# Attention backward with cached K and V: gradient stores moved to the SyncE queue, and three quarters of K transposed by DMA

## The chip, the cores and the metric

The kernel runs on one core of a Trainium2 chip. The metric is the device time of one execution in microseconds; for the kernel before, it is the median of three runs. A profile is one further execution, recorded by the hardware profiler. Engines are called PE (TensorE matmul), PEld (TensorE weight load), DVE (VectorE), ACT (ScalarE), POOL (GpSimd) and SP (SyncE, which here only issues DMAs). "SPq" in a profile line is SP's instruction queue.

## The reference

Two independent attention blocks, A and B, share one output gradient, and each is computed forward and backward. Everything is bfloat16: 8 batches of 96 queries, model width 640, 32 heads of width 128, 512 cached keys and values per head and batch.

```python
def ref(x, k_cache, v_cache, wq, wo):            # for A and for B
    q = (x @ wq).reshape(B, Sq, H, Dh).transpose(0, 2, 1, 3)
    scores = einsum("bhqd,bhkd->bhqk", q, k_cache) * Dh ** -0.5
    p = softmax(scores)
    o = einsum("bhqk,bhkd->bhqd", p, v_cache)
    return o.transpose(0, 2, 1, 3).reshape(B, Sq, H * Dh) @ wo
out = concatenate([ref(A...), ref(B...)], -1)
# returned: out, and for each block the gradients of x, k_cache, v_cache, wq, wo
```

The gradients of k_cache and v_cache are as large as the caches: 8 x 32 x 512 x 128 values each, 33.6 MB, twice for two blocks. Loading K and V and storing dK and dV is most of the traffic.

## The kernel before

Work is cut into 2 blocks x 32 heads x 8 batches = 512 items, one item being one head of one batch. The items run through a software pipeline of *ticks*: in each tick, PE, DVE, ACT and POOL each do one stage of several neighbouring items. An emitter collects closures under a tick and a slot, sorts them, and calls them in that order, so the order of the program is written out by hand; the compiler behind it may still reorder instructions, except those wrapped in `pinned(...)`, which keep the order of the program on their engine. `OFF` gives the tick of each stage relative to the item's own tick: K load -5, V load -3, K^T -3, V^T 0, the score matmul S (stage s2) 3, dV (s4) 4, dP (s6) 6, dK (s7) 7, dQ (s8) 8.

Loads, transposes and stores go by pairs of batches (`NB = 2`), 256 KB each. The steps that the change and the prediction touch:

- `c_ld` (L266) loads K_sb (7 buffers) or V_sb (5 buffers) of a pair from SP. A K buffer comes free when stage s8 of the pair seven earlier has read it.
- `c_xt` (L275) transposes a loaded pair by a crossbar DMA from SP, into VT (4 buffers) for every pair and into KT (2 buffers) for those pairs whose K^T is not made on PE.
- `c_s1` (L285, L287) makes K^T of one item on PE instead: four 128 x 128 transposes into PSUM (kT_ps) and a copy by DVE into KT_pe. `k_on_pe` chooses: pairs 0 and 2 of a head's four, all of head 0 of a block, and all of head 1 of the first block.
- `c_s2a` (L298) multiplies Q with K^T into S_ps; softmax follows on DVE (L300), ACT (L310), DVE (L320) and POOL (L329, P_sb).
- `c_s4` (L389) and `c_s7` (L432) make dV and dK of an item in PSUM, and ACT copies each (L392, L435) into dV_sb or dK_sb, which hold a pair and have 3 buffers each.
- `c_st` (L398) stores such a pair. It is issued by POOL, whose DMAs go through the software queue, and it is pinned there together with POOL's P_sb (L329) and prod (L407). A dV store is emitted two ticks after the dV stage of the pair's first item, a dK store likewise.
- `c_s6` (L417) reads V^T for dP.

Around these stand work per head (projections, transposes of weights, dwo and dwq: L210, L216, L243, L258, L455, L470, L490), whose weight loads and gradient stores POOL issues, and group work (L512): after every five or six heads, the output and dx products of the group are spread over 9 ticks each.

Of the kernel before, what the change touches and what calls it, by code (L numbers as in the profile page):

```python
# [44 lines left out]
OFF = dict(ldk=-5, ldv=-3, kt=-3, vt=0, s2=3, s3=3, s4=4, s5=5, s6=6, s7=7, s8=8)  # L45
# [5 lines left out]
SLOTS = dict(LOAD=0, S2A=5, S2B=5.5, S1=6, S8=10, S7=20, S5=30, S4=40, S6=50, S3A=52, S3B=53, S5B=54, HEAD=SL_HEAD, GRP=SL_GRP)  # L51


def build_block(tc, em, tick0, blk, x, kc, vc, wq, wo, g_all, out_all, dx, dk, dv, dwq, dwo, ident, ones, pools, HG=6, first=True, groups=None):
    nc = tc.nc
# [7 lines left out]
    KC = Sk // 128  # L63
    NB = 2
# [38 lines left out]
    SB = {}  # L103
    HS = pools["HS"]
    CS = pools["CS"]
# [5 lines left out]
    def pinned(ins):  # L111
        return tc.keep_in_program_order(ins)
# [68 lines left out]
    def pA(h):  # L181
        def f():
            start = first and h == 0
            if h % 2 == 0:
                wq_p = hd.tile([128, DC, 256], BF16, name="wq_p", bufs=2)
                with nc.allow_non_contiguous_dma(reason="wq slice of two heads"):
                    if start:
                        nc.sync.dma_start(wq_p[:], wq_v[:, :, h * 128:(h + 2) * 128])
                    else:
                        pinned(nc.gpsimd.dma_start(wq_p[:], wq_v[:, :, h * 128:(h + 2) * 128]))  # L190
            else:
                wq_p = HS[(blk, h - 1)]["wq_p"]
            HS[(blk, h)] = dict(wq_p=wq_p, wq_h=wq_p[:, :, (h % 2) * 128:(h % 2 + 1) * 128])
        return f

    def pA2(h):
        def f():
            wo_h = hst.tile([128, D], BF16, name="wo_h", bufs=HG + 3)
            ld = nc.gpsimd.dma_start(wo_h[:], wo[h * 128:(h + 1) * 128, :])
            if not (first and h == 0):  # L200
                pinned(ld)
            HS[(blk, h)]["wo_h"] = wo_h
        return f
# [23 lines left out]
    def pC(h, which, si):  # L227
        def f():
            st = HS[(blk, h)]
            (t0, w) = tsplits[si]  # L230
            if which == 0:
                dst = st["QT_h"]
                lhs = lambda c: st["wq_h"][:, c, :]
                rhsT = S["xT"]
                sc = scale
            else:
                dst = st["dOT_h"]
                lhs = lambda c: st["woT_h"][:, c * 128:(c + 1) * 128]
                rhsT = S["gT"]
                sc = None  # L240
            q_ps = bank([128, w], F32, "q_ps")
            for c in range(DC):
                nc.tensor.matmul(q_ps[:], lhs(c), rhsT[:, c, t0:t0 + w], start=(c == 0), stop=(c == DC - 1))  # L243
            evac(EV["pC%d%d" % (which, si)], dst[:, t0:t0 + w], q_ps[:], sc)
        return f
# [16 lines left out]
    def c_ld(h, b, n, bufs):  # L262
        def f():
            src = kc if n == "K" else vc
            X = kvp.tile([128, NB, KC, 128], BF16, name=n + "_sb", bufs=bufs)
            nc.sync.dma_start(X[:], src[b:b + NB, h].rearrange("b (p c) d -> p b c d", c=KC))  # L266
            for i in range(NB):
                st = CS.setdefault((blk, h, b + i), {})
                st[n + "_sb"], st[n + "_all"] = X[:, i], X
        return f  # L270

    def c_xt(h, b, name, bufs):
        def f():
            XT = kvp.tile([128, NB * KC, 128], BF16, name=name, bufs=bufs)
            nc.sync.dma_start_transpose(XT[:], CS[(blk, h, b)][name[0] + "_all"][:].rearrange("p a c d -> p (a c d)"))  # L275
            for i in range(NB):
                CS[(blk, h, b + i)][name] = XT[:, i * KC:(i + 1) * KC].rearrange("p c k -> p (c k)")
        return f
# [116 lines left out]
    def c_st(h, b, which):  # L395
        def f():
            dst = dv if which == "v" else dk
            pinned(nc.gpsimd.dma_start(dst[b - 1:b + 1, h].rearrange("b (p c) d -> p b (c d)", c=KC), SB.pop((blk, h, b // 2, which))[:]))  # L398
        return f

    def c_s5b(h, b):
# [144 lines left out]
    NTS = len(tsplits)  # L546

    def k_on_pe(h, b):
        return (b // NB) % 2 == 0 or h == 0 or (first and h == 1)

    SX = pools["SX"]
    for g in range(NG):
        h0 = GH0[g]
        for hh in range(groups[g]):
            h = h0 + hh
            c0t = tick0 + h * B
            if not (first and h == 0):
                em.add(c0t + HK["pA"], 54.6, pA(h))
                em.add(c0t + HK["pA2"], 54.6, pA2(h))
            em.add(c0t + HK["pB"], SL_HEAD, pB(h))  # L560
            fh = first and h == 0
            p0, p1, d1, d0, late = HK["pC0"], HK["pC1"], HK["pD1"], HK["pD0"], 0
            if fh:
                p1, d1, d0, late = [3, 3], 3, 4, 7
            elif h == 0:
                p0, p1, d1, d0, late = [-2, 2], [0, 3], 3, 4, 7
            for si in range(NTS):
                em.add(c0t + p0[min(si, 1)], SL_HEAD, pC(h, 0, si))
                em.add(c0t + p1[min(si, 1)], SL_HEAD + late, pC(h, 1, si))
            em.add(c0t + d1, SL_HEAD + (8 if late else 0), pD(h, 1))  # L570
            em.add(c0t + d0, SL_HEAD, pD(h, 0))
            for b in range(B):
                ct = c0t + b
                if b % NB == 0:
                    em.add(tick0 - 12 if first and h == 0 and b == 0 else ct + OFF["ldk"], SLOTS["LOAD"], c_ld(h, b, "K", 7))
                    em.add(ct + OFF["ldv"], SLOTS["LOAD"], c_ld(h, b, "V", 5))
                    if not k_on_pe(h, b):
                        em.add(ct + OFF["kt"], SLOTS["LOAD"] + 1, c_xt(h, b, "KT", 2))
                    em.add(ct + OFF["vt"], SLOTS["LOAD"] + 1, c_xt(h, b, "VT", 4))
                if k_on_pe(h, b):  # L580
                    em.add(ct + 2, SLOTS["S1"], c_s1(h, b))
                em.add(ct + OFF["s2"], SLOTS["S2A"], c_s2a(h, b))
                em.add(ct + OFF["s2"], SLOTS["S2B"], c_s2b(h, b))
                em.add(ct + OFF["s3"], SLOTS["S3A"], c_s3a(h, b))
                em.add(ct + OFF["s3"], SLOTS["S3B"], c_s3b(h, b))
                em.add(ct + OFF["s5"], SLOTS["S5B"], c_s5b(h, b))
                if b % 2 == 1:
                    em.add(ct + OFF["s4"] + 1, 54.3, c_st(h, b, "v"))
                    em.add(ct + OFF["s7"] + 1, 54.3, c_st(h, b, "k"))
                em.add(ct + OFF["s4"], SLOTS["S4"], c_s4(h, b))  # L590
                for i, o in enumerate(("s8", "s7", "s5", "s4")):
                    SX.setdefault(ct + OFF[o], [None] * 4)[i] = (blk, h, b)
                em.add(ct + OFF["s6"], SLOTS["S6"], c_s6(h, b))
                em.add(ct + OFF["s7"], SLOTS["S7"], c_s7(h, b))
            hk = HK if first or h < H - 1 else dict(HK, qA0=13, qB=[14, 15], qA1=16, qD=[(19, 0, 2), (19, 2, 4), (19, 4, 5)])
            em.add(c0t + hk["qA0"], SL_HEAD, qA(h, 0))
            for di in range(len(wsplits)):
                em.add(c0t + hk["qB"][di], SL_HEAD + 1, qB(h, di))
            em.add(c0t + hk["qA1"], SL_HEAD, qA(h, 1))
            for (k_, c_lo, c_hi) in hk["qD"]:  # L600
                if c_lo < DC and h % 2 == 1:
                    em.add(c0t + k_, SL_HEAD + 2, qD(h, c_lo, min(c_hi, DC)))
        cLg = tick0 + (h0 + groups[g] - 1) * B + B - 1
        gs0 = max(3, (GSPREAD0 * groups[g]) // HG)
        gs1 = max(3, (GSPREAD1 * groups[g]) // HG)
        if not first and g == NG - 2:
            gs0, gs1 = 9, 9
        if g == 0:
            em.add(cLg + OFF["s5"] - 2, SL_LOAD, setup_acc)
        subs = [(0, t, gi) for t in range(TT) for gi in range(len(gsplits))] + [(1, t, gi) for t in range(TT) for gi in range(len(gsplits))]  # L610
        n_out = TT * len(gsplits)
        for i, (which, t, gi) in enumerate(subs):
            if which == 0:
                tk = cLg + OFF["s5"] + 2 + (i * gs0) // n_out
            else:
                tk = cLg + OFF["s8"] + 2 + gs0 - 3 + ((i - n_out) * gs1) // n_out
            em.add(tk, SL_GRP, gU(g, which, t, gi))
# [124 lines left out]
```

## Time and profile before

| | before |
|---|---|
| time, three runs | 1693.32, 1705.34, 1706.98 us (median 1705.34) |
| span of the profiled execution | 1699.8 us (the page gives no other time of that execution) |
| mean granted TensorE clock | 0.998 |
| busy: PE, ACT, DVE, POOL | 1675.7, 1405.2, 1329.8, 1040.3 us |
| moved by DMA | 423.05 MB, 249 GB/s in the mean |
| of these on the hardware queue (SP) / the software queue (POOL) | 242.08 MB / 177.35 MB |
| dV and dK stores, from issue to landing | 5.2 and 5.3 us (median), 256 each |
| K and V loads, from issue to landing | 4.9 to 5.3 us (median), 128 of each kind |
| V^T and K^T by DMA, from issue to landing | 6.1 us (256) and 5.2 us (122) |

A row of the profile's groups reads: line, engine, operation, what it writes and reads, shapes, count, then busy us in all and mean ns of one, then idle time before it and who ended it. A busy PE counts the whole duration of pipelined matmuls, which overlap, so the cost of one is better read from start to start. The DMA share counts a packet from its start to its end, also while it waits for another queue's packets; it can exceed 1.

### The profile page before, as it was taken

To read this page: it belongs to the slowest core of one execution; us is meant where nothing else is said; L and a number is where in the kernel's file an instruction comes from. 1 tells how busy PE (TensorE), PEld (TensorE's weight loads), DVE (VectorE), ACT (ScalarE), POOL (GpSimd) and SP (SyncE) were. 2 spreads that over 40 slices of the span, in tenths; PEclk is the share of its full clock that TensorE was granted. 3 is DMA by queue.
4 is the path that set the end of the run, shared out by engine and by line. 5 is a ranking of instruction groups with operands and counts; after the bars stand their busy time and mean duration, and the time that the engine had idled before them with its cause. 6 is when DMAs were issued, how large, how long until landed. Compare 5 with 4: busy or idle time off the path is not lost.

```text
span 1699.8 us, 56567 instructions
## 1 busy us (share of the span) xinstructions
PE 1675.7 (99%) x22024; PEld 1343.8 (79%) x22024; DVE 1329.8 (78%) x3052; ACT 1405.2 (83%) x3518; POOL 1040.3 (61%) x1747
## 2 busy tenths in 40 slices
PE   8999999999999999999999999999999999999999
PEld 7877778778778778777778877887788778778876
DVE  6887678878788878787778876787788778878877
ACT  6998889869869869878768998897799679878975
POOL 3676567646647647656566764675576557656754
PEclk9999999999999999999999999999999999999999
DMA  9999999999999999999999999999899989999994
GB/s 256 252 259 250 258 225 260 262 242 243 262 221 252 268 238 259 225 251 237 281 256 269 273 270 248 238 289 248 218 261 276 237 221 261 281 217 240 263 247 141
DMA packets 600429, 423.05 MB, mean 249 GB/s; under 512 B 419360, under 2 KB 557984, under 8 KB 600160
## 3 DMA queue, kind: packets, MB, share of 16 engines
q1 hardware_dynamic: 546576, 242.08, 72.2%
q0 software_dynamic: 53584, 177.35, 32.7%
q8 instruction: 173, 2.83, 0.7%
q14 instruction: 96, 0.79, 0.2%
HBM read 161.09 MB, written 159.12 MB: 188 GB/s over the span
## 4 chain that ended last, share of the span: by engine, by line
PE 89%; DMA 4%; ACT 3%; issue 1%; DVE 1%; POOL 0%; SPq 0%; DVEq 0%; ACTq 0%; POOLq 0%
PE q_ps L243 12%; PE o_ps L512 12%; PE dwo_ps L470 6%; PE dV_ps L389 6%; PE dK_ps L432 6%; PE S_ps L298 6%; PE dP_ps L417 6%; PE dwq_ps L490 6%; PE x_ps L340 5%; PE x_ps L365 5%; PE dst_ps L346 5%; PE x_ps L359 5%; PE kT_ps L285 3%; PE n_ps L258 3%; PE nat_ps L455 2%; DMA VT<-V_sb 1%
## 5 line engine op out<-in xcount | busy, mean ns | idle before, releaser
L329 POOL TENSOR_SCALAR P_sb<-E_sb,rinv 96x512 bf16<-96x512 bf16 x512 | 352.6, 689 | 567.8 <-DVE rinv L320 559.2
L310 ACT ACTIVATE E_sb<-S_ps,negm 96x512 bf16<-96x512 f32 x512 | 351.0, 686 | 187.6 <-DVE negm L300 181.9
L421 DVE SCALAR_TENSOR_TENSOR dS_sb<-dP_ps,dl_ps,P_sb 96x512 bf16<-96x512 f32 x512 | 382.1, 746 | 60.9 <-PE dl_ps L419 54.6
L300 DVE TENSOR_REDUCE negm<-S_ps 96x1 f32<-96x512 f32 x512 | 347.6, 679 | 50.9 <-PE S_ps L298 46.6
L435 ACT ACTIVATE dK_sb<-dK_ps 128x512 bf16<-128x512 f32 x512 | 302.1, 590 | 63.4 <-PE dK_ps L432 56.5
L392 ACT ACTIVATE dV_sb<-dV_ps 128x512 bf16<-128x512 f32 x512 | 311.6, 609 | 0.0
L378 ACT ACTIVATE PT_sb<-x_ps 128x384 bf16<-128x384 bf16 x512 | 253.1, 494 | 0.0
L512 PEld LDWEIGHTS <-OD 128*128 128x128 bf16 x1536 | 132.2, 98 | 100.4 <-issue 1.0
L398 POOL DMA_DIRECT2D out_dram<-dV_sb x256 | 194.9, 761 | 11.8 <-issue 8.6
L398 POOL DMA_DIRECT2D out_dram<-dK_sb x256 | 195.0, 762 | 9.1 <-issue 4.4
L389 PE MATMUL dV_ps<-dOnat_h,P_sb 96*128 96x128 bf16 x2048 | 198.2, 219 | 0.8 <-DVE dOnat_h L160 0.6
L417 PE MATMUL dP_ps<-VT,dOT_h 128*96 128x512 bf16 x512 | 195.4, 382 | 3.0 <-DMA VT<-V_sb 3.0
L432 PE MATMUL dK_ps<-Qnat_h,dS_sb 96*128 96x128 bf16 x2048 | 198.1, 219 | 0.1
L407 POOL TENSOR_TENSOR prod<-OD,dOT_h 128x96 bf16<-128x96 bf16 x512 | 184.2, 360 | 13.8 <-ACT OD L375 12.6
L348 DVE COPY dST_sb<-dst_ps 128x384 bf16<-128x384 bf16 x512 | 177.1, 346 | 10.5 <-PE dst_ps L346 10.3
L365 PE MATMUL x_ps<-ident,P_sb 96*128 96x96 bf16 x2048 | 172.0, 205 | 0.8 <-POOL P_sb L329 0.3
L359 PE MATMUL x_ps<-PT_sb,V_sb 128*128 128x96 bf16 x2048 | 172.3, 206 | 0.2 <-ACT PT_sb L378 0.2
L346 PE MATMUL dst_ps<-ident,dS_sb 96*128 96x96 bf16 x2048 | 172.3, 206 | 0.2 <-DVE dS_sb L421 0.2
L340 PE MATMUL x_ps<-dST_sb,K_sb 128*128 128x96 bf16 x2048 | 171.0, 206 | 1.3 <-ACT dK_sb L435 0.8
L375 ACT ACTIVATE OD<-x_ps 128x192 bf16<-128x192 f32 (+1 forms) x515 | 167.9, 326 | 3.9 <-PE x_ps L340 3.9
L320 DVE RECIPROCAL rinv<-rowsum 96x1 f32<-96x1 f32 x512 | 79.9, 156 | 106.0 <-ACT E_sb L310 100.4
L340 PEld LDWEIGHTS <-K_sb 128*128 128x128 bf16 x2048 | 131.1, 98 | 25.1 <-issue 1.6
(84 smaller groups left out, 3744.4 us busy)
## 6 DMA issues: line engine op xcount, KB each, us to landing
out_dram<-dV_sb POOLq DMA_DIRECT2D x256, 256.0 KB, 5.2
out_dram<-dK_sb POOLq DMA_DIRECT2D x256, 256.0 KB, 5.3
K_sb<-in_A_k_cache_dram SPq DMA_DIRECT2D x128, 256.0 KB, 5.3
V_sb<-in_A_v_cache_dram SPq DMA_DIRECT2D x128, 256.0 KB, 5.2
K_sb<-in_B_k_cache_dram SPq DMA_DIRECT2D x128, 256.0 KB, 5.0
V_sb<-in_B_v_cache_dram SPq DMA_DIRECT2D x128, 256.0 KB, 4.9
out_dram<-dwo_sb POOLq DMA_DIRECT2D x63, 160.0 KB, 4.8
out_dram<-dwq_sb POOLq DMA_DIRECT2D x31, 320.0 KB, 6.1
```

The costliest lines, as they stand in the source:

```text
L300: nc.vector.tensor_reduce(negm[:], S_ps[:], axis=AX.X, op=ALU.max, negate=True)
L310: nc.scalar.activation(E_sb[:], st["S_ps"][:], ACT.Exp, bias=st["negm"][:], scale=1.0, accum_out=rowsum[:])
L329: pinned(nc.gpsimd.tensor_scalar(P_sb[:], st["E_sb"][:], st["rinv"][:], 0.0, op0=ALU.mult, op1=ALU.add))
L340: nc.tensor.matmul(dQT_ps, st["K_sb"][:, c, :], st["dST_sb"][:, c * Sq:(c + 1) * Sq], start=(c == 0), stop=(c == KC - 1))
L389: nc.tensor.matmul(dV_ps[:, c * 128:(c + 1) * 128], P_sb[:, c * 128:(c + 1) * 128], hs["dOnat_h"][:, b * 128:(b + 1) * 128], start=True, s ...
L392: nc.scalar.activation(SB[(blk, h, b // 2, "v")][:, b % 2], dV_ps[:], ACT.Identity, scale=1.0)
L398: pinned(nc.gpsimd.dma_start(dst[b - 1:b + 1, h].rearrange("b (p c) d -> p b (c d)", c=KC), SB.pop((blk, h, b // 2, which))[:]))
L417: nc.tensor.matmul(dP_ps[:], hs["dOT_h"][:, tok], st["VT"], start=True, stop=True)
L421: nc.vector.scalar_tensor_tensor(dS_sb[:], dP_ps[:], dl_ps[:, 0:1], st["P_sb"][:], op0=ALU.subtract, op1=ALU.mult)
L432: nc.tensor.matmul(dK_ps[:, c * 128:(c + 1) * 128], dS_sb[:, c * 128:(c + 1) * 128], hs["Qnat_h"][:, b * 128:(b + 1) * 128], start=True, s ...
L435: nc.scalar.activation(SB[(blk, h, b // 2, "k")][:, b % 2], dK_ps[:], ACT.Identity, scale=1.0)
L512: nc.tensor.matmul(o_ps[:], src[:, t * 128:(t + 1) * 128], rhs, start=(hh == 0), stop=(hh == groups[g] - 1))
```

## The change

The dV and dK stores are issued by SP, on its hardware queue, instead of POOL. In the emitter they get a slot right behind the loads and transposes of their tick, and loads, transposes and stores are all pinned, so SP issues them in the written order: V load, K load, K^T, dK store, V^T, dV store for each pair. `k_on_pe` keeps only pair 0 of a head on PE (and the same whole heads as before), so three quarters of a head's K^T come by DMA, 183 transposes instead of 122, and KT gets three buffers.

```diff
@@ c_ld
-            nc.sync.dma_start(X[:], src[b:b + NB, h].rearrange("b (p c) d -> p b c d", c=KC))
+            pinned(nc.sync.dma_start(X[:], src[b:b + NB, h].rearrange("b (p c) d -> p b c d", c=KC)))
@@ c_xt
-            nc.sync.dma_start_transpose(XT[:], CS[(blk, h, b)][name[0] + "_all"][:].rearrange("p a c d -> p (a c d)"))
+            pinned(nc.sync.dma_start_transpose(XT[:], CS[(blk, h, b)][name[0] + "_all"][:].rearrange("p a c d -> p (a c d)")))
@@ c_st
-            pinned(nc.gpsimd.dma_start(dst[b - 1:b + 1, h].rearrange("b (p c) d -> p b (c d)", c=KC), SB.pop((blk, h, b // 2, which))[:]))
+            pinned(nc.sync.dma_start(dst[b - 1:b + 1, h].rearrange("b (p c) d -> p b (c d)", c=KC), SB.pop((blk, h, b // 2, which))[:]))
@@ k_on_pe
-        return (b // NB) % 2 == 0 or h == 0 or (first and h == 1)
+        return b // NB == 0 or h == 0 or (first and h == 1)
@@ the loop over items
                     if not k_on_pe(h, b):
-                        em.add(ct + OFF["kt"], SLOTS["LOAD"] + 1, c_xt(h, b, "KT", 2))
+                        em.add(ct + OFF["kt"], SLOTS["LOAD"] + 1, c_xt(h, b, "KT", 3))
                     em.add(ct + OFF["vt"], SLOTS["LOAD"] + 1, c_xt(h, b, "VT", 4))
...
                 if b % 2 == 1:
-                    em.add(ct + OFF["s4"] + 1, 54.3, c_st(h, b, "v"))
-                    em.add(ct + OFF["s7"] + 1, 54.3, c_st(h, b, "k"))
+                    em.add(ct + OFF["s4"] + 1, SLOTS["LOAD"] + 1.5, c_st(h, b, "v"))
+                    em.add(ct + OFF["s7"] + 1, SLOTS["LOAD"] + 1.5, c_st(h, b, "k"))
```

## The prediction

> **What bounds the kernel now.** I read the page's busy line, the row of slices and the chain first, then the waits of PE, ACT and the SP queue, then windows of single heads.
>
> ```profile
> PE 1675.7 (99%) x22024; PEld 1343.8 (79%) x22024; DVE 1329.8 (78%) x3052; ACT 1405.2 (83%) x3518; POOL 1040.3 (61%) x1747
> ...
> DMA  9999999999999999999999999999899989999994
> ...
> PE 89%; DMA 4%; ACT 3%; issue 1%; DVE 1%; POOL 0%; SPq 0%; DVEq 0%; ACTq 0%; POOLq 0%
> ```
>
> PE sets the time: it is busy for 99% of the span and holds 89% of the chain. POOL, from which the change takes work, is on no path. The DMA row of 9s is a warning for a change that adds DMA work, but a weak one: a packet counts as busy while it waits, and packets of two queues overlap.
>
> ```profile
> PE dP_ps L417 <- DMA VT<-V_sb: 3.0, 2, 2.4
> ...
> PE S_ps L298 <- DMA KT<-K_sb: 2.1, 1, 2.1
> ```
>
> PE's waits (total us, times, longest) name a late transpose for only 5.1 us in all. So DMA is hidden now; how much room is left must be read from stretches of the run.
>
> The 64 heads are not alike. Taking the first dP matmul of each head as its mark, a head without group work (L512) takes 21 or 24 us in turn, and the two heads that carry it take about 33 and 30. Windows of two neighbouring heads and, first, of the stretch in which only the SP queue moves data (columns: window, its length, then busy us and instructions of PE, PEld, DVE, ACT, POOL, then PE clock, DMA share, GB/s):
>
> ```profile
> 17.00:24.00 7.00, 6.07 (x83) 4.74 (x81) 5.45 (x13) 5.14 (x14) 1.72 (x3) 1.00 1.16 331
> ...
> 949.90:970.90 21.00, 20.94 (x302) 17.28 (x300) 17.79 (x43) 20.85 (x55) 16.08 (x27) 1.00 1.17 281
> 970.90:995.10 24.20, 24.20 (x341) 20.53 (x339) 20.13 (x46) 21.87 (x56) 16.11 (x27) 1.00 1.18 278
> ```
>
> Three things are to be seen. In the 21 us head ACT is busy for 20.85 of 21.00 us, so there PE has a second engine at its side that is just as full. The DMA share reads 1.16 to 1.18 in all three, while the rate goes from 278 to 331 GB/s, so the share tells nothing and the rate does. And 331 GB/s came with one ring alone, loads and transposes back to back.
>
> **Step 1: what is taken from PE.** K^T came from PE for pairs 0 and 2 of each head's four; now only for pair 0, with heads 0 and 1 of the first block and head 0 of the second wholly on PE as before. That is 30 + 31 = 61 pairs, each 2 items x 4 transposes: 488 transposes with their weight loads, and 122 copies on DVE. PE's order is otherwise the same, instruction for instruction, but for two transitions. What one transpose costs is read from start to start, since matmuls overlap:
>
> ```profile
> 902.03 0.39 PE L285 MATMUL kT_ps<-ident,K_sb 128*128 128x128 bf16 x4
> 902.26 0.33 PE L340 MATMUL x_ps<-dST_sb,K_sb 128*128 128x96 bf16 x4
> ```
>
> Four take 0.23 us, 57.5 ns each: 488 x 57.5 = 28.1 us. The low bound is the chain's 3% for L285: 51 us over 1072 transposes, 48 ns, 23 us. The group's 97 ns (104.0 us over 1072) would give 47, but it counts overlapping durations, so I leave it out. I take 28.1.
>
> **Step 2: where PE is not alone.** 17 of the touched heads take about 21 us. Each loses 8 x 57.5 = 0.46 us of PE work, but ACT, from which nothing is removed, has 0.15 us to spare. I count 0.15 there: 17 x 0.31 = 5.3 us of the gain are not had (bounds: 0 if ACT's lag is carried into the next, slower head; 7.8 if nothing is had there). The DVE copies, 122 x 411 ns = 50 us, cost and bring nothing: DVE is idle for 22% of the span and beside PE.
>
> **Step 3: POOL and the stores.** 512 issues at 761 ns, 390 us, leave POOL. Worth nothing: PE waited 0.3 us for P_sb in the whole run. The stores themselves stay as large. Their margin is the three buffers of dV_sb and dK_sb. From a store's landing to the ACT copy that writes its buffer anew I find 7.1 us (dV) and 5.9 us (dK) in the mean, 3 to 5 in the 21 us heads. ACT waited 3.1 us for such a store in all. On SP the dK store comes after V load, K load and K^T of its tick, about 2.5 us of issues, where POOL now issues it 4.2 us after the copy's end. So its margin stays about the same as long as SP keeps pace.
>
> **Step 4: the SP queue, where everything now stands.** The row for one pair of batches becomes: V load, K load, K^T, dK store, V^T, dV store. Two edits meet here. K^T now follows the *next* pair's K load, so its own K was issued a pair earlier. Before, it stood behind its own K load and SP stood still for it:
>
> ```profile
> SPq L275 <- DMA K_sb<-in_A_k_cache_dram: 169.4, 57, 9.0
> SPq L275 <- DMA K_sb<-in_B_k_cache_dram: 152.0, 61, 4.8
> ```
>
> 321 us in 118 waits, 2.7 us for each K^T before; most of that goes. In return the stores wait on SP for ACT's copies, and behind them V^T, the next V load and the next K load wait, and for these PE. The copies were made in the tick before, so I take these waits as nil; one tick (2.6 us) late in every pair would be the upper end, and six ticks of lead for K^T and V^T (some 16 us in the fast heads, of which landing takes 4 to 8) cover it.
>
> SP's issue time, per head after the change, from its rows' medians: 4 V^T x 1.44 + 3 K^T x 1.25 + 4 K loads x 0.48 + 4 V loads x 0.58 + 8 stores. A 256 KB store from SP is not in the trace. The nearest are the 160 KB stores at the end (0.33 us) and the same-sized loads (0.48 to 0.62, up to 1.1 when the queue is full). I take 0.55: 5.8 + 3.8 + 1.9 + 2.3 + 4.4 = 18.2 us; bounds 16.4 and 22.6. PE needs (21.0 + 24.2) / 2 - 0.46 = 22.1 us for the mean fast head. It fits, narrowly at the upper end.
>
> **Step 5: the transfers.** Per head 16 copies and 7 transposes of 0.262 MB and 0.66 MB of weights and their gradients: 6.68 MB, or 302 GB/s at 22.1 us. That is more than the 278 to 281 of the two windows and less than the 331 of the one-ring stretch. There a V^T landed 3.8 us after its issue, against 7.3 (median) in four fast heads with stores on POOL's queue beside it. I take the value near 331, because after the change all but 0.66 MB per head go in one ring, as there, and cost 0 on PE; the other end is the slow rival. Stores from SP at the run's end do not look slower than loads (160 KB landed in 1.8 to 2.1 us).
>
> The Trainium skill speaks against the move: "DMA: Bandwidth & Descriptors", section "Issuing engines are not separate DMA queues", says that DMAs of all issuers share the same 16 engines and interleave, so that a second issuer saves only sequencer time. By it the move gains no bandwidth and gives up that saving; if the rate stayed at its present value too, the sum would be the slow rival's. The two windows above, at 281 and 331 GB/s, do not read like one rate for both arrangements.
>
> **Sum.** 28.1 - 5.3 = 22.8 us off the profiled span of 1699.8: 1677. The page has only the span; the median of the three runs, 1705.3, is 5.5 us above it. I keep that distance: 1682 us. With the bounds of steps 1 and 2, gains of 15 to 28 us, this case alone spans 1677 to 1690.
>
> **Rivals.** *Slow: the one ring falls behind in the fast heads.* If the rate there stays at the 267 GB/s of the window over four fast heads (926 to 1016 us), a head needs 6.68 / 0.267 = 25.0 us against 22.1. Some 41 heads are fast, in 11 stretches; each stretch can first use up the 3.5 us margin of the stores. 41 x 2.9 - 11 x 3.5 = 80 us: 1682 + 80 = 1762 us. ACT then waits at L435 and L392 for landed stores, PE behind it. It begins below 290 GB/s (23.0 us per head) and eats the whole gain at 283. For it: margins already shrink through each fast stretch now (V^T lands 20 us ahead of its dP matmul after group heads, 3 to 8 at the end of a stretch), and SP has one more transpose and eight stores to issue. Against it: that shrinking went with SP's waits on K, which the new order takes away, and the stretch at 331.
>
> *No gain that can be told: ACT becomes the bound.* If in all 41 fast heads the saving is lost to ACT and to stores that SP issues a little late, only the 20 or so heads with group work keep 0.46 us each: 9 us, 1696 us. For it: ACT at 20.85 of 21.00. Against: 21.87 of 24.20 in the other half of the fast heads.
>
> **How the numbers follow.** Forecast 0.50, no gain 0.17, slow 0.33. A measurement of this kernel tells about 1% from no change: faster means below 1688, slower above 1722. The slow case is a slide from 1700 to 1762, so most of it lies above 1722. The range goes from 1668 (the full 28 us and the 5 us of late transposes, at the median's distance and a little noise) to 1750, which leaves out the worst part of the slow case.
>
> **What would show it.** Right: L285 with 584 transposes, PE waits on KT, VT and on ACT still a few us; SP's waits for K_sb far below 321 us; V^T landing near 4 to 5 us in fast heads and 300 GB/s there; the 21 us heads shortened by less than the 24 us ones. Wrong: ACT dV_sb or dK_sb waiting on DMA for tens of us, or PE on KT or VT, with fast heads at 24 us or more; or SP waiting long on ACT at the stores.

## The result, and the profile after

| | before | changed |
|---|---|---|
| median (lowest to highest), four runs each | 1699.78 us (1693.32 to 1706.98) | 1680.93 us (1672.74 to 1685.22) |
| span of the profiled execution | 1699.8 us | 1679.9 us |
| mean granted TensorE clock | 0.998 | 0.999 |
| moved by DMA | 423.05 MB, 249 GB/s | 439.02 MB, 261 GB/s |

For the kernel before, a fourth run (1694.21 us) has joined the three known earlier and moved the median from 1705.34 to 1699.78 us. The ratio of the times is 0.9859 (95% interval 0.9811 to 0.9907): faster by 0.9 to 1.9%. The profiled execution itself took 1681.76 us, 1.9 us above its span. First the page of the changed kernel: instruction counts of the engines, DMA, its two queues, and the chain by engine.

```profile
PE 1648.9 (98%) x21536; PEld 1317.8 (78%) x21536; DVE 1279.4 (76%) x2930; ACT 1397.8 (83%) x3518; POOL 665.4 (40%) x1235
...
DMA packets 763150, 439.02 MB, mean 261 GB/s; under 512 B 483776, under 2 KB 753472, under 8 KB 762880
...
q1 hardware_dynamic: 750256, 392.32, 98.8%
q0 software_dynamic: 12624, 43.10, 8.6%
...
PE 78%; ACT 11%; DMA 5%; issue 3%; DVE 2%; SPq 0%; POOL 0%; ACTq 0%; DVEq 0%; POOLq 0%
```

PE lost exactly the 488 transposes and DVE the 122 copies. But PE is 31 us short of the span where it was 24.1 us short before, and ACT and DMA have risen in the chain from 3% and 4% to 11% and 5%: something new holds PE up now and then. The waits (total us, times, longest) say what:

```profile
ACT dK_sb L435 <- DMA out_dram<-dK_sb: 24.1, 22, 2.7
...
PE x_ps L340 <- ACT dK_sb L435: 5.1, 6, 1.1
```

No wait of PE for KT or VT at L298 or L417 is left. In its place ACT stands 22 times at the dK copy until an old dK store has landed, and PE stands behind ACT. Such a stand in the changed kernel, on ACT (first line) and on PE (the others; columns: start, us, engine, line, operation, idle before it):

```profile
296.75 0.60 ACT L435 ACTIVATE dK_sb<-dK_ps 128x512 bf16<-128x512 f32 x1 [1.01 <-DMA out_dram<-dK_sb]
...
296.40 0.55 PE L258 MATMUL n_ps<-ident,dOT_h 128*96 128x128 bf16 x7
297.40 0.38 PE L285 MATMUL kT_ps<-ident,K_sb 128*128 128x128 bf16 x4 [0.44 <-ACT dK_sb L435]
298.00 0.33 PE L340 MATMUL x_ps<-dST_sb,K_sb 128*128 128x96 bf16 x4 [0.22 <-ACT PT_sb L378]
```

ACT loses 1.01 us and PE at once 0.44 and 0.22 us. The SP queue's own waits for a loaded K have gone, 321 us before and 3.9 us now:

```profile
SPq L275 <- DMA K_sb<-in_B_k_cache_dram: 2.5, 4, 1.3
SPq L275 <- DMA K_sb<-in_A_k_cache_dram: 1.4, 4, 0.5
```

### The profile page after: what moved, and what is told of

It is laid out like the page before. It is cut to its first block, busy times and chain, and to the rows that moved or that the text cites. A ratio compares the mean times of both kernels' runs of the same rounds, so it can differ in the third digit from the quotient of the medians.

```text
span 1679.9 us, 56195 instructions
## 1 busy us (share of the span) xinstructions
PE 1648.9 (98%) x21536; PEld 1317.8 (78%) x21536; DVE 1279.4 (76%) x2930; ACT 1397.8 (83%) x3518; POOL 665.4 (40%) x1235
## 2 busy tenths in 40 slices
DMA packets 763150, 439.02 MB, mean 261 GB/s; under 512 B 483776, under 2 KB 753472, under 8 KB 762880
## 4 chain that ended last, share of the span: by engine, by line
PE 78%; ACT 11%; DMA 5%; issue 3%; DVE 2%; SPq 0%; POOL 0%; ACTq 0%; DVEq 0%; POOLq 0%
PE o_ps L512 12%; PE q_ps L243 11%; PE dwq_ps L490 6%; PE dK_ps L432 5%; PE dV_ps L389 5%; PE dP_ps L417 5%; PE S_ps L298 5%; DMA out_dram<-dK_sb 5%; PE dst_ps L346 4%; PE x_ps L365 4%; PE x_ps L359 4%; PE x_ps L340 4%; PE dwo_ps L470 4%; PE n_ps L258 3%; ACT dK_sb L435 2%
## 5 line engine op out<-in xcount | busy, mean ns | idle before, releaser
L435 ACT ACTIVATE dK_sb<-dK_ps 128x512 bf16<-128x512 f32 x512 | 306.4, 598 | 101.2 <-PE dK_ps L432 66.0
L392 ACT ACTIVATE dV_sb<-dV_ps 128x512 bf16<-128x512 f32 x512 | 315.8, 617 | 0.5 <-DMA out_dram<-dV_sb 0.4
L378 ACT ACTIVATE PT_sb<-x_ps 128x384 bf16<-128x384 bf16 x512 | 257.2, 502 | 0.0
L407 POOL TENSOR_TENSOR prod<-OD,dOT_h 128x96 bf16<-128x96 bf16 x512 | 185.2, 362 | 31.3 <-ACT OD L375 29.7
L417 PE MATMUL dP_ps<-VT,dOT_h 128*96 128x512 bf16 x512 | 195.4, 382 | 0.0
L375 ACT ACTIVATE OD<-x_ps 128x192 bf16<-128x192 f32 (+1 forms) x515 | 171.7, 333 | 3.9 <-PE x_ps L340 3.9
L298 PE MATMUL S_ps<-KT,QT_h 128*96 128x512 bf16 x366 | 138.7, 379 | 0.4 <-ACT dK_sb L435 0.4
L243 PE MATMUL q_ps<-gT,woT_h 128*128 128x512 bf16 (+1 forms) x640 | 136.9, 325 | 1.2 <-ACT gT L157 0.6
```

The costliest lines, as they stand in the source:

```text
L392: nc.scalar.activation(SB[(blk, h, b // 2, "v")][:, b % 2], dV_ps[:], ACT.Identity, scale=1.0)
L417: nc.tensor.matmul(dP_ps[:], hs["dOT_h"][:, tok], st["VT"], start=True, stop=True)
L435: nc.scalar.activation(SB[(blk, h, b // 2, "k")][:, b % 2], dK_ps[:], ACT.Identity, scale=1.0)
```

## The experiments

Two of the theories below were formed from the trace after: (1) the time is right as a sum, but the K^T part brings its saving only because order and queue make room for it; (2) what the ring can't keep up with comes out first at the dK stores, which have the least margin, and this takes back much of the saving. The rivals were that the two parts are independent, and that the dK waits cost nothing. In the texts quoted here, "the time of the kernel before" is that of runs on the same chip; its median differs by some 10 us between chips (1699.78 to 1710.15 us), so the ratio is the number to compare.

### The two parts alone

`kt_only`: only K^T and its third buffer; stores on POOL in slot 54.3, nothing pinned on SP.

> Only the K^T part of the change: three quarters by DMA and three KT buffers; stores stay on POOL, SP's order is the compiler's as before. Theory (SP stands still for the K load just issued before each K^T, 2.7 us each, and stores on a second ring slow the transposes): a third K^T per head adds some 4 us of SP time to each fast head, stretches of four run out of their margin of 3 to 8 us, PE waits on KT and VT for 50 to 120 us in all; 1720 to 1790 us. Rival (the gain is K^T alone; where the stores are issued does not matter): as the full change, 1676 to 1686 us, PE waits on KT and VT under 10 us.

Measured: 1742.39 us as the median of the three runs that the ratio counts (1747.42 us with a fourth, the longest), ratio 1.0185 (1.0101 to 1.0269). Alone this part makes the kernel slower. PE waits for late transposes and SP stands for K. The profiled execution is that longest one, with a span of 1760.3 us, so the sizes of the waits hold for it alone:

```profile
PE S_ps L298 <- DMA KT<-K_sb: 48.4, 34, 3.6
PE dP_ps L417 <- DMA VT<-V_sb: 13.8, 14, 1.8
...
SPq L275 <- DMA K_sb<-in_B_k_cache_dram: 267.7, 92, 7.3
SPq L275 <- DMA K_sb<-in_A_k_cache_dram: 251.9, 90, 5.6
```

`stores_only`: the stores on SP and the pinned order; K^T stays half and half:

```diff
-        return b // NB == 0 or h == 0 or (first and h == 1)
+        return (b // NB) % 2 == 0 or h == 0 or (first and h == 1)
-                        ... c_xt(h, b, "KT", 3))
+                        ... c_xt(h, b, "KT", 2))
```

> Only the stores on SP and the pinned order; K^T as before, half on PE, two KT buffers. Theory: PE has all its work back, so no gain from that; late transposes (about 5 us) go; 1692 to 1702 us, SP waits for K_sb near nothing. Rival (the move of the stores frees something worth time by itself): under 1688 us. Rival (one ring is too slow): over 1710 us with ACT waiting on dK_sb stores.

Measured: 1686.84 us, ratio 0.987 (0.9828 to 0.9912), span 1685.2 us. The part that takes nothing from PE brings nearly as much as the whole change; the two intervals overlap, so these times alone do not show what K^T adds. My expected time was too high, and what came is the figure of the first rival: I held the late transposes of the kernel before for 5 us, and its late transfers cost some 10 us in the profiled execution (below). Two edits are in this run, the queue of the stores and the pinned order; which of them does it with half of K^T on PE was not tried.

`kt_only` and `stores_only` don't add up to the change: 1.85% slower and 1.3% faster alone, 1.4% faster together. Theory 1 holds, the two parts depend on each other.

### Which half of the move makes room: the queue or the order?

`pool_stores`: the change with its pinned loads and transposes, but the stores issued by POOL, in slot 54.3.

> The full change with its pinned order of loads and transposes, but the stores back on POOL's queue in their old slot. Theory that the order of SP decides: like the full change or a little better, 1672 to 1685 us, since the dK stores leave SP's queue. Theory that the single ring decides (331 against 281 GB/s): fast heads of 23.8 us, 1700 to 1720 us, with V^T landing near 7 us and PE waits on KT or VT.

Measured: 1749.64 us, ratio 1.0255 (1.0193 to 1.0316), slower than either theory gave.

```profile
PE S_ps L298 <- DMA KT<-K_sb: 51.1, 26, 5.4
...
VT<-V_sb SPq DMA_TRANSPOSE x256, 6.8
KT<-K_sb SPq DMA_TRANSPOSE x183, 6.2
```

The second and third line are the DMA issues with their median landing: 6.8 and 6.2 us, against 5.0 and 4.9 in the changed kernel, with the same order on SP. Issuing a V^T takes SP 2.61 us here (median), against 1.51. The rate does not explain this. Heads 40 to 43 and 46 to 49 of `pool_stores` (columns as in the prediction's windows):

```profile
1090.20:1180.64 90.44, 89.96 (x1248) 75.03 (x1250) 72.97 (x168) 85.24 (x219) 64.17 (x108) 1.00 1.13 278
1243.25:1345.18 101.93, 93.64 (x1247) 76.87 (x1249) 75.54 (x171) 85.86 (x217) 63.85 (x108) 0.97 1.14 236
```

The first four heads run without a wait of PE, at 278 GB/s, where the changed kernel has 266. In the other four PE waits for K^T, and they show 236 GB/s against 274 because they take longer for nearly the same data (24.1 and 24.8 MB). So with three quarters of K^T by DMA, stores on POOL's queue and in POOL's slot turn the gain into a loss; why SP's transposes are issued and land later beside them isn't shown, only that they do.

`unpinned`: the whole change, with only the two `pinned(...)` around loads and transposes taken away.

> The full change without the pins on loads and transposes; stores stay pinned on SP. The compiler then puts K^T right behind V^T and dK between the V load and the K load. Theory: K^T still has about a pair's time behind its K load, K waits stay small; within 6 us of the full change, 1675 to 1687 us. Rival (the fixed order is what makes it work): SP's waits for K_sb return to over 100 us and the time is over 1695 us.

Measured: 1793.85 us, ratio 1.0494 (1.0432 to 1.0556), the slowest of all. The compiler leaves mostly V^T and one or two stores between a K load and its own K^T, where the written order has five or six steps between them, and it puts the dK store mostly between V load and K load. SP stands again:

```profile
SPq L275 <- DMA K_sb<-in_B_k_cache_dram: 131.8, 85, 3.8
SPq L275 <- DMA K_sb<-in_A_k_cache_dram: 120.5, 80, 4.0
...
ACT dK_sb L435 <- DMA out_dram<-dK_sb: 59.9, 40, 5.0
ACT dV_sb L392 <- DMA out_dram<-dV_sb: 43.3, 27, 4.1
```

Once the stores share SP's queue, a stand for K also holds up stores, and 103 us of waits on ACT follow. Queue and order are both needed for three quarters of K^T.

`kt_two`: the changed kernel with `c_xt(h, b, "KT", 2)`.

> The changed kernel with two KT buffers instead of three. Theory (the third buffer is needed because three K^T of a head follow each other): with two, pair 3's K^T writes the buffer that the score matmuls of pair 1 read two to three ticks later, and since SP's order is pinned, V^T, stores and loads behind it stand too; SP shows tens to hundreds of us of waiting at the K^T for PE at L298, and the time is 1710 to 1770 us. Rival (six ticks of lead are enough to swallow the stand): the time stays at 1678 to 1690 us with SP waiting but PE not.

Measured: 1766.33 us, ratio 1.0339 (1.031 to 1.0369). The time is that of the theory, and so is the stand on SP: its idle gaps in front of a K^T add up to 214 us (22 in the changed kernel), and it stands up to 11.6 us at a time at a transpose (4.9 in the changed kernel). The way to PE is another than lateness of K^T itself. PE never waits for KT; the stores queued behind it come too late:

```profile
SPq L275 <- PE o_ps L512: 74.1, 10, 11.6
...
ACT dK_sb L435 <- DMA out_dram<-dK_sb: 95.9, 67, 3.5
```

So the third KT buffer is no extra: without it the change is 3.4% slower than the kernel before.

### What the dK store waits cost

`full_again` is the changed kernel once more, as the base on the chip of the next three.

> The full change once more, beside the next three on one chip. All theories: a ratio of 0.98 to 0.99 to the kernel before; ACT waits 20 to 30 us for dK stores.

Measured: 1683.99 us, ratio 0.9844 (0.9762 to 0.9926), 28.7 us of dK store waits on ACT.

`dk_first`: the dK store goes ahead of the loads of its tick.

```diff
-                    em.add(ct + OFF["s7"] + 1, SLOTS["LOAD"] + 1.5, c_st(h, b, "k"))
+                    em.add(ct + OFF["s7"] + 1, SLOTS["LOAD"] - 1, c_st(h, b, "k"))
```

> The full change with the dK store ahead of its tick's V and K loads instead of behind K^T, so issued about 2 us sooner. Theory (what eats the rest of the gain is the margin of the three dK_sb buffers: ACT waits for a landed store, PE behind it, about 15 us): ACT's waits on dK stores fall below 10 us, and the time by 8 to 15 us below the full change. Rival (the ring itself is full in the fast heads, the store is only where it shows): the wait moves to KT, VT or dV_sb, time within 4 us of the full change. Rival (SP waits for ACT at the store and holds the loads back): slower by 5 us or more.

Measured: 1686.39 us, ratio 0.9874 (0.9803 to 0.9945), no better. The wait moved:

```profile
ACT dV_sb L392 <- DMA out_dram<-dV_sb: 18.5, 15, 3.5
PE S_ps L298 <- DMA KT<-K_sb: 3.1, 2, 2.5
ACT dK_sb L435 <- DMA out_dram<-dK_sb: 2.5, 2, 1.7
```

What dK gains in the queue, dV and K^T lose. SP's queue is behind; the order only chooses who is late.

`dk_four`: one more dK buffer, its room taken from a staging tile.

```diff
-... name="dK_sb", bufs=3)
+... name="dK_sb", bufs=4)
-            stp=P(name="stp", bufs=5),
+            stp=P(name="stp", bufs=4),
```

> The full change with four dK_sb buffers instead of three (and four instead of five staging tiles, to make room). Theory of the dK margin: two more ticks of time for each dK store, ACT's waits on it near 0, PE without waits in the fast heads, 12 to 18 us below the full change. Rival (the ring is full): the lag goes on growing through a stretch and shows at dV_sb, KT or VT; gain under 5 us.

Measured: 1670.74 us, ratio 0.9788 (0.9717 to 0.9859). The intervals of this and of `full_again` overlap, so it was run again on another chip:

> The changed kernel with four dK_sb buffers (and four staging tiles instead of five), once more on this chip, as the base for the two kernels beside it. Theory (the dK copy's wait for the store before it costs about 13 us): ratio 0.975 to 0.982 to the kernel before, no wait at L435 for a dK store. Rival (the earlier gain over the changed kernel was scatter): ratio 0.983 to 0.990.

Measured: 1672.25 us, ratio 0.9787 (0.9754 to 0.9821). The dK waits are gone, some waiting has moved to dV (13.1 us in the first run, 9.7 in this one).

`both_four`: four buffers for dV_sb too; the room comes from one KT_pe buffer instead of two and three staging tiles.

> The changed kernel with four dV_sb and four dK_sb buffers; room for them from one KT_pe buffer instead of two and three staging tiles instead of five. Theory (what is lost is the stores' margin, not bandwidth): with 13 us of dV store waits gone too, 1660 to 1670 us and heads of 20.7 and 23.8 us without stalls. Rival (the ring is at its limit, and a deeper buffer only hands the lateness on to K^T and V^T): 1668 to 1680 us, PE waiting for KT or VT. A single KT_pe buffer may cost PE a little at pair 0, up to 64 x 0.1 us.

Measured: 1666.72 us, ratio 0.9755 (0.9728 to 0.9782), span 1662.7 us: the best version, faster than the kernel before by 2.2 to 2.7%, and its interval lies apart from that of the change in its first measurement (0.9811 to 0.9907), though not from that of `full_again` (0.9762 to 0.9926). No store wait is left on ACT, and PE is 19.3 us short of the span:

```profile
PE 1643.4 (99%) x21536; PEld 1315.8 (79%) x21536; DVE 1278.8 (77%) x2930; ACT 1396.3 (84%) x3518; POOL 664.6 (40%) x1235
...
PE S_ps L298 <- DMA KT<-K_sb: 3.2, 1, 3.2
```

The second line, from its waits, is a first sign of the rival: one K^T came 3.2 us late. The margin is nearly used up there too.

`all_dma`: no K^T on PE but in the three whole heads (`return h == 0 or (first and h == 1)`), four KT buffers, one KT_pe buffer.

> The full change taken further: all four pairs of a head by DMA (four KT buffers, one KT_pe buffer), 62 transposes more, 496 PE transposes (28 us of PE) less. Theory (the transfers are at the edge of what the one ring carries in the fast heads): some 0.9 to 1.2 us of DMA more per head against 0.46 us less PE time; waits on dK stores grow to 60 us or more and the time rises to 1690 to 1720 us. Rival (PE is still the bound): another 15 us faster, 1660 to 1670 us.

Measured: 1709.41 us, ratio 1.0018 (0.9978 to 1.0058). Another 61 pairs of K^T off PE give back everything:

```profile
ACT dK_sb L435 <- DMA out_dram<-dK_sb: 65.0, 37, 4.6
...
PE x_ps L340 <- ACT dK_sb L435: 36.7, 21, 4.0
```

### Does ACT cap the 21 us heads?

`dk_four_relief`: `dk_four` with the copy into woT_h moved from ACT to DVE (`EV` with `pB0="dve"`).

> Four dK_sb buffers, and the copy into woT_h (L212, 0.72 us per head) moved from ACT to DVE. Theory of the prediction (ACT caps what a 21 us head can save): these heads get shorter by up to 0.1 to 0.3 us, 2 to 5 us in all against the kernel with four dK_sb buffers alone. Rival (ACT's lag is carried into the next, slower head, so nothing is capped): 20.7 us heads as before, same time within 2 us, or slower where DVE delays the softmax.

Measured: 1669.71 us, ratio 0.978 (0.9746 to 0.9813), the same as `dk_four_again` (0.9787). The 21 us heads stay at 20.7 us, as the rival had it. The 24 us heads go from 23.8 to 23.6 us, which I hadn't foreseen; 12 such heads are 2 us.

## Why the prediction was right, and where it was not

The total was 1682 and 1680.93 us came, and much of that nearness is luck. The gain from the median known then was to be 23 us; from the four-run median it is 18.9. Two parts that I had put at nothing nearly cancelled. The lengths of the heads, counted from 0, from the first dP matmul of one head to that of the next, show it (us, one profiled execution each; the last head is counted to its last dP matmul):

| head | before | stores_only | both_four | changed |
|---|---|---|---|---|
| 4 | 28.3 | 24.1 | 23.8 | 23.8 |
| 5 | 23.2 | 21.1 | 20.6 | 22.6 |
| 11 | 21.1 | 21.1 | 20.6 | 23.0 |
| 25 | 21.1 | 21.1 | 20.6 | 20.7 |
| 29 | 24.4 | 21.1 | 20.7 | 20.7 |
| 31 | 28.6 | 24.4 | 26.0 | 28.2 |
| 36 | 24.1 | 25.2 | 27.0 | 24.4 |
| 37 | 21.1 | 21.1 | 20.6 | 23.8 |
| 60 | 24.1 | 24.1 | 23.8 | 23.8 |
| sum of heads 1 to 63 | 1634.4 | 1620.4 | 1598.6 | 1615.8 |

Read from left to right: without the kernel before's late transfers 14.0 us less; with K^T taken from PE and no store waits 21.8 us less; with the change's own store waits 17.2 us more. In all 18.6 us, where I had 22.8. An execution scatters: by the ratio of the times, 0.987, `stores_only` gains some 22 us.

**Steps 1 and 2, PE's work: 22.8 us predicted, 21.8 us from `stores_only` to `both_four`.** As a sum right, its two terms less so; the 21.8 are also net of 1.6 and 1.7 us that heads 31 and 36 lost in `both_four`. The median head saves 0.42 us, 53 ns for each of eight transposes instead of 57.5. The 21 us heads save 0.42 as well (0.40 in the changed kernel), not the 0.15 that I allowed. ACT doesn't cap them. There were two faults. The windows that I read were cut 10.7 us late against the heads, as their times were counted from another zero than the heads', so that what I called the 21 us head held parts of two heads. Cut right, heads 24 and 25 read as follows, first before, then in the changed kernel (columns as in the prediction's windows):

```profile
641.48:665.61 24.13, 24.13 (x336) 20.31 (x334) 19.96 (x46) 21.99 (x57) 16.34 (x28) 1.00 1.10 245
665.61:686.68 21.07, 21.01 (x306) 17.50 (x304) 17.94 (x43) 20.73 (x54) 15.80 (x27) 1.00 1.15 270
```

```profile
630.69:654.48 23.79, 23.75 (x328) 19.96 (x326) 18.71 (x44) 21.79 (x56) 10.28 (x19) 1.00 1.20 275
654.48:675.15 20.67, 20.56 (x298) 17.12 (x296) 17.25 (x40) 20.52 (x55) 10.26 (x19) 1.00 1.14 264
```

ACT had 0.34 us to spare in head 25, not 0.15. And it stayed as full, 20.52 of 20.67 us, in a head that got shorter: an engine with its queue full over one head may be working off what the longer head before it left. That was my lower bound of 0 for this step, and the nearer one. The 24 us heads saved only 0.34 of the 0.46 us; with the woT_h copy off ACT (`dk_four_relief`) they are 0.16 us shorter still, which points to ACT there.

**The kernel before: lateness counted at 5.1 us of waits, worth some 10 us.** This gain I had left out of the sum and put, at 5 us, into the low end of the range. One V^T, 2.4 us late at head 4, made that head 4.1 us longer. Windows of 3.4 us in the kernel before, over the wait and behind it:

```profile
122.80:126.20 3.40, 1.03 (x17) 0.81 (x14) 1.33 (x5) 1.72 (x6) 1.73 (x3) 1.00 0.89 290
126.20:129.60 3.40, 3.40 (x24) 2.49 (x23) 1.83 (x4) 1.51 (x3) 0.00 (x0) 0.55 1.07 300
129.60:133.00 3.40, 3.40 (x43) 2.89 (x42) 2.41 (x6) 2.06 (x5) 1.81 (x3) 0.94 1.13 208
```

Behind the wait stands a stretch at clock 0.55, in which PE is busy all the time and gets through 24 matmuls. A K^T that was 2.1 us late costs head 5 the same 2.1 us. Head 29, with 3.1 us of dK store waits on ACT, lost 3.3 us, and the start of the second block (head 31) 4.1 us. The last is not due to the change: PE waits there for `ld_tmp`, 2.7 us before and 2.6 us after, followed by the half clock, and `stores_only` merely didn't meet it. Without it, 9.9 of the 14.0 us are left.

**Steps 3 and 4, stores and SP's queue.** K waits gone, as predicted; a 256 KB store takes SP 0.54 and 0.57 us (median), I had 0.55; SP's idle gaps in front of the 512 stores are 63 us in all, so the waits for ACT's copies were rightly taken as small. The step that failed is step 4's sum of issue times, 18.2 us of SP in a fast head of 22.1, and with it step 3's "its margin stays about the same as long as SP keeps pace". I had added up medians, and SP did not keep pace.

In the 37 heads (of 2 to 62) that took under 26.2 us before, one V^T takes SP 1.94 us in the mean of the changed kernel, a K^T 1.47, a K or V load 0.51, a dK store 0.67 and a dV store 0.76: 21.9 us for the row of a head. Between two instructions stand another 0.09 us, 2 us for 23 of them. Together that is 24 us. SP issues for 89% of the time in these heads and stands longer than 0.15 us between two instructions for only 4% of it; in the kernel before it was 59% and 34%. So the dK stores are issued later and later through a stretch: 2 to 5 us after their copy in heads 57 and 58, 8 to 11 in heads 60 and 61, while from issue to landing they take 3 to 6 us in these four heads. What lengthens an issue is in part told by the trace: with three of SP's transfers still under way a V^T takes 1.51 us to issue in the mean, with five 2.05, with six 2.66, and its buffer was free each time. That points to the transfers, but no run separates them from SP's own work.

The time from a dK store's landing to the copy that reuses its buffer three pairs later, in us for the four pairs of each head of one stretch of the changed kernel:

| head | dK margin | least margin of V^T, K^T |
|---|---|---|
| 57 (group work) | 9.3, 10.2, 9.8, 5.2 | 17.2, 13.1 |
| 59 | 3.7, 3.0, 4.1, 0.1 | 12.1, 11.1 |
| 60 | 0.6, 0.1, 0.8, 0.1 | 9.9, 6.7 |
| 61 | 0.4, 0.1, 3.1, 6.0 | 6.8, 4.3 |

At 0.1 the copy started the moment the store had landed: it had waited. In `stores_only`, with a transpose less in each head, the least margins of heads 59, 60 and 61 are 3.1, 4.0 and 4.2 us. In `both_four` the same stores land up to 4.2 us too late for three buffers, and the fourth takes that up. This is a lag that grows by a few us in a stretch, not a queue that has broken down. I costed it at 0, and it was 17.2 us (of which 2.1 are in head 31). The ratios, 0.9859 and 0.9755, put the same at 1.0% of the time before, some 17 us.

**Step 5, the rate.** It failed as I worked it: over no 90 us of any run, about four fast heads, was 331 GB/s reached, nor the needed 302 (294 at most, in `unpinned`). Over heads 46 to 49 the changed kernel moved 274 GB/s and `both_four` 268, without a wait of PE for a transpose. The mistake was to ask for the rate in each head. Group heads leave SP time (9.4 of 29.7 us idle in head 57), and the lead gathered there is spent in the fast heads; what counts is by how much the queue falls behind in one stretch, against the smallest margin in it. Nor did 281 against 331 GB/s tell the two arrangements apart: with the stores on POOL's queue, `pool_stores` moved 390 GB/s over 7 us (908 to 915 us) and 289 over 90 us (1111 to 1201 us), the changed kernel 375 (3 to 10 us) and 286 (892.5 to 982.5 us).

Of the rule in the Trainium skill, "DMA: Bandwidth & Descriptors", section "Issuing engines are not separate DMA queues", the runs agree with the part on sharing, as SP's transposes land later beside POOL's stores, but not with the conclusion: an issuer's choice is worth far more than sequencer time here, 1749.64 us with the stores on POOL's queue against 1680.93 and 1683.99 us on SP's. The page "Advanced Engine Details and Errata", section "X-Bar Transpose (TRN2)", calls transposes as fast as other DMAs, at an expected 350 to 400 GB/s. The changed kernel's land 4.9 and 5.0 us after the start of their issue, where loads of the same size take 4.0 to 4.3; but the issue itself takes 1.24 and 1.51 us, a load's 0.42 and 0.45, and from its end the transposes take 3.4 and 3.3 us, the loads 3.6 and 3.8. So as to speed this case agrees; no stretch with transposes alone tests the rate.

**The distance from span to time.** Kept at 5.5 us. By the same reckoning, median less span of the profiled execution, the changed kernel has 1.0 us, and the kernel before has none with its fourth run: the 5.5 were scatter. By luck they made up for a span that came 2.9 us longer than predicted.

**The rivals.** The slow rival is real but came in its mildest form, as a queue whose row is not issued in time; that the ring's rate is the limit behind it isn't shown. Its place (ACT at L435, PE behind it) is where the change lost its 17 us, and its full price turns up one step further on, in `all_dma` (65.0 us of dK waits) and `kt_two`. Its threshold, "eats the whole gain at 283" GB/s, was wrong, since I granted a stretch only the 3.5 us of store margin and not the 10 to 20 us of lead of the transposes. ACT as the bound did not come about. Of the signs named beforehand, L285 has its 584 transposes, K waits and V^T landings are as predicted, the 300 GB/s did not come, the 21 us heads were shortened by more than the 24 us ones and not by less, and one sign of the wrong case, ACT waiting tens of us for dK stores, is there with 24.1 us: enough to take back most of what the K^T part saves, and too little to turn the result.

## What to carry to other kernels

Before moving transfers to a queue, write down the margin of each kind of transfer over a stretch of the run, from landing to use and from landing to reuse of its buffer: the smallest breaks first, and a buffer more for that one (here 2 KB per partition for dK and dV each) can be worth as much as the whole edit. In a queue with a fixed order, a wait anywhere is passed on to all that stands behind it, so issue first what is already ready, and count every buffer that an instruction in that queue may have to wait for. When you add up a queue's issue times, take means from the busy stretches and the time between instructions, not medians of the whole run. And undo each half of a change by itself: here one half alone gave nearly the whole gain, and the other alone was a loss.

## What the runs showed of the hardware

- **A short wait of PE can cost more than itself.** After a wait of 2.4 us the granted clock was 0.55 over the next 3.4 us. "TensorE: Matmul & The Clock Gate", section "What's actually happening", tells of half speed after an idle window of about 3.4 us; here 2.4 us without a matmul, with PE busy for 1.03 of 3.40 us, were enough. In the fourteen profiles of this case, start and end of the run left out, there are 63 stretches at half clock, each 3.41 us long or two or three times that, and in the 3.41 us ahead of each PE was busy for 1.76 us at most. Not every wait is followed by one: behind the 3.2 us of `both_four` in head 36 and the 2.1 us of the kernel before in head 5 the clock stayed at 1.00. In `pool_stores` the mean clock was 0.985: of its 1748.2 us some 26 us worth of clock are missing, on top of the waits themselves.
- **The same transposes are slower beside stores on POOL's queue, and not for want of rate.** With the same order on SP, V^T landed in 6.8 us with 256 KB stores on POOL's queue and in 5.0 with them on SP's own; SP took 2.61 and 1.51 us to issue it. The highest rates over 7 and over 90 us were no lower with two queues (390 and 289 GB/s) than with one (375 and 286). Whether packet sizes, the two queues' turns or the transposes' own needs do this was not tried.
- **What stays open:** whether the ring or SP itself lengthens SP's issues in the fast heads; why one K^T came 3.2 us late in head 36 of `both_four`; and why the 24 us heads save less than the others, beyond the hint of the woT_h copy.
